# Rebuilding the head of a Fourier-mixing and leaky-ReLU kernel: even and odd rows, small first weights, a fixed order

## The chip, the cores and the metric

The kernel runs on one core of a Trainium2 chip. The metric is the device time of one execution in microseconds, as the median of several runs. Beside it there is one profiled execution, whose span goes from the first to the last instruction; all durations of single instructions come from that execution.

## The reference

The input is x of 8 batches, 3008 rows and 256 columns. It is Fourier-transformed along the rows and along the columns, the real part is kept, and the 24064 resulting rows of 256 values go through two weight matrices with a leaky ReLU between them:

```python
X = np.fft.fft(x, axis=1)
X = np.fft.fft(X, axis=2)
x = X.real.astype(np.float32).reshape(B * S, D)
h = x @ w_in                   # 256 x 2048
g = np.maximum(0.01 * h, h)
return (g @ w_out).astype(np.float32)   # 2048 x 256
```

The weights arrive as float64, everything else as float32.

## The kernel before

**Folding the transform.** Real Fourier transforms have mirror symmetries, and the kernel uses them to shrink the products. For one batch, `load_x` brings x into one tile `xt` with two halves h, two mirrored copies, seven row groups and 256 columns. The first four row groups are even rows, the last three odd rows (`NI = [4, 3]`). `fold_rows` adds the mirrored rows of one half and forms sums and differences of mirrored columns; `fold_halves` adds and subtracts the two halves. All of this is VectorE work (with a small ScalarE copy and a GpSimd memset for the edge columns). `sequence` then multiplies the folded rows with sine and cosine tables on TensorE, four products for the even rows and three for the odd rows, and `butterfly` combines the results on VectorE into `mix0` and `mix1`, the mixed activations. One such pair is a unit (batch, parity of the output row); there are 16 units, with 753 or 752 columns. Column 128 of x has no mirror, the Nyquist column: `fold_nyquist`, `nyquist` and `spread` transform it for all batches at once and send the row through DRAM to all partitions as `nb`.

**The column transform is folded into the weights.** `fold_w_in` multiplies w_in with a table, so that `wf` holds the transformed weights, and `wn`, one scalar for each hidden value, the Nyquist weights. `wn` is a row of `wf` that is turned into columns by a trip through DRAM (`spread_wn`). The float64 weights are first converted to float32 by the class `Weights`: five VectorE operations and two ScalarE operations for each tile of 128 x 512.

**The blocks.** Each unit is cut into three blocks of 251 or 250 columns, and for each block there are eight steps f over the hidden values, two hidden blocks of 128 in each. `up` makes cos_ps and sin_ps (four products), VectorE adds the Nyquist term (`cos`, lines 496 to 498), forms sum and difference (`g`, lines 500 and 501), ScalarE applies the leaky ReLU (line 502). `down` adds g times w_out into PSUM, three steps later (`lag = 3`). The first two blocks are "plain": they use w_out as it is, eight products a step (`down_plain`). All later blocks use seven products on combinations `wt` of w_out, made by `combine_w_out` on GpSimd, and combinations `s` of g, also made on GpSimd.

**The order.** A scheduler places the instructions of each engine from the order in which the program writes them; each engine then works through its list in that order. SyncE issues nearly all transfers from one queue. The head runs from line 595 on: load and convert the first and third 512 columns of w_in, fold them, send wn through DRAM, fold the Nyquist column, load and fold x of batch 0, transform unit 0; then the plain steps, two at a time, with the rest of the weights converted between them. In the plain steps of before, step f works on the hidden blocks f and 8 + f, which is why the head needs columns 0 to 511 and 1024 to 1535 first.

Of the kernel before, what the change touches and what calls it, by code (L numbers as in the profile page):

```python
# [201 lines left out]
def tile_fnet_leaky_relu(  # L202
# [24 lines left out]
    def load_x(b, q=None):  # L227
        t = xp.tile([P, 2, 2, NT, D], F32, tag="x", bufs=1, name="xt")
        for h in range(2):
            (q or nc.sync).dma_start(t[:, h], x[b, :, h])  # L230
        return t
# [3 lines left out]
    def fold_rows(t, h):  # L235


        a, z = t[:, h, 0], t[:, h, 1]
        nc.vector.tensor_tensor(a, a, z, op=ALU.add)
        lo, hi = a[:, :, 1:P], a[:, :, P + 1 : D]  # L240
        nc.vector.tensor_tensor(z[:, :, P + 1 : D], lo, hi, op=ALU.subtract)
        nc.vector.tensor_tensor(z[:, :, 1:P], lo, hi, op=ALU.add)
        nc.scalar.copy(z[:, :, 0:1], a[:, :, 0:1])
        nc.gpsimd.memset(z[:, :, P : P + 1], 0.0)

    def fold_halves(b, t):

        a, z = t[:, :, 0], t[:, :, 1]
        nc.vector.tensor_tensor(a[:, 0], z[:, 0], z[:, 1], op=ALU.add)
        nc.vector.tensor_tensor(a[:, 1], z[:, 0], z[:, 1], op=ALU.subtract)  # L250
        zs[b] = t
# [19 lines left out]

    quarters = {}
# [9 lines left out]
    wn_dram = dram.tile([2, F // 2], F32, name="wn_dram")  # L282
# [7 lines left out]
    class Weights:  # L290
# [7 lines left out]
        def __init__(self, src, dst):  # L298
            n = len(parts)
            tag, bufs = (("o", 2), ("e", 2), ("raw", 1))[n % 3]  # L300
            self.raw = work.tile([P, 2 * WN], F32, tag=tag, bufs=bufs, name="raw")
            self.dst = dst
            self.f64 = src.dtype != F32
            raw = self.raw if not self.f64 else self.raw.bitcast(src.dtype)
            nc.sync.dma_start(raw[:, 0 : src.shape[1] * src.shape[2]].rearrange("p (c n) -> p c n", c=src.shape[1]), src)  # L305
            parts.append(self)
# [4 lines left out]
        def begin(self):  # L311
            if not self.f64:
                return
            hi = self.word(I32, 1)
            self.power = work.tile([P, WN], F32, tag="power", bufs=2, name="power")
            man, power = self.dst, self.power
            man_i, power_i = man.bitcast(I32), power.bitcast(I32)
            v = nc.vector
            v.tensor_scalar(man_i, in0=hi, scalar1=0xFFFFF, scalar2=0x100000, op0=ALU.bitwise_and, op1=ALU.bitwise_or)
            v.tensor_scalar(power_i, in0=hi, scalar1=20, scalar2=0x7FF, op0=ALU.logical_shift_right, op1=ALU.bitwise_and)  # L320
            nc.scalar.activation(power, power_i, ACT.Relu, scale=-1.0, bias=inf[:, 0:1])
            nc.scalar.activation(power_i, power, ACT.Relu, scale=-(2.0**23), bias=inf[:, 1:2])

        def end(self):
            if not self.f64:
                nc.vector.tensor_copy(self.dst, self.raw[:, 0:WN])
                return
            hi, lo = self.word(I32, 1), self.word(U32, 0)
            man, power = self.dst, self.power
            man_i, power_i = man.bitcast(I32), power.bitcast(I32)  # L330
            v = nc.vector
            v.scalar_tensor_tensor(man, in0=lo, scalar=2.0**-32, in1=man_i, op0=ALU.mult, op1=ALU.add)
            v.scalar_tensor_tensor(power_i, in0=hi, scalar=-(2**31), in1=power_i, op0=ALU.bitwise_and, op1=ALU.bitwise_or)  # L333
            v.scalar_tensor_tensor(man, in0=man, scalar=2.0**-20, in1=power, op0=ALU.mult, op1=ALU.mult)
# [3 lines left out]
    def convert(made):  # L338
        for w in made:
            w.begin()  # L340
        for w in made:
            w.end()

    def load_w_in(f0):
        n, made = w_in.shape[1] // F, []
        for a in range(2):
            w = work.tile([P, WN], F32, tag="win", bufs=4, name="win")
            src = w_in[a * P : (a + 1) * P, n * f0 : n * (f0 + WN)].rearrange("p (c n) -> p c n", c=1)
            made.append(Weights(src, w))
        return made  # L350

    def fold_w_in(f0, made):

        for w in range(2):
            pt = up_ps()
            for a in range(2):
                nc.tensor.matmul(pt, lhsT=feat_sb[:, a, w * P : (w + 1) * P], rhs=made[a].dst, start=(a == 0), stop=(a == 1))  # L357
            nc.scalar.copy(wf[:, w, f0 : f0 + WN], pt)

    def spread_wn(f0):  # L360


        row = wn_dram[:, f0 : f0 + WN]
        nc.scalar.dma_start(row.rearrange("(o h) n -> o h n", o=1), wf[0:1, 1].rearrange("o (h n) -> o h n", h=2)[:, :, f0 : f0 + WN])
        at = f0 // P

        def rest():
            for h in range(2):
                nc.scalar.dma_start(wn[:, h * NH + at : h * NH + at + WN // P], row[h].rearrange("(q p) -> p q", p=P))  # L369
        return rest  # L370

    def load_w_out(f):
        made = []
        for h in range(2):
            at = (h * NH + f) * P
            src = w_out[at : at + WB * P, :].rearrange("(c p) d -> p c d", p=P)
            made.append(Weights(src, wo[:, h, f : f + WB, :].rearrange("p c d -> p (c d)")))
        return made
# [51 lines left out]
    def dft(u, blk):  # L430
# [3 lines left out]
        if c == 1:  # L434
            rows = zs[b][:, 1 - blk, 0, :, blk * P : (blk + 1) * P]
        else:
            rows = quarters.pop((b, blk))
# [12 lines left out]
    def fold_nyquist():  # L450
        nc.vector.tensor_tensor(nyb, nya, nyb, op=ALU.add)
        nc.vector.tensor_tensor(nya[:, 0], nyb[:, 0], nyb[:, 1], op=ALU.add)
        nc.vector.tensor_tensor(nya[:, 1], nyb[:, 0], nyb[:, 1], op=ALU.subtract)

    def nyquist(c):
# [8 lines left out]
        def rest():  # L464
            t = work.tile([P, UW[0]], F32, tag="mix0", bufs=2, name="nyq")
            butterfly(t, sums, B, 0, c)
            nc.sync.dma_start(nyq_dram[:, c, 0 : UW[c]], t[0:B, 0 : UW[c]])
        return rest
# [7 lines left out]


# [6 lines left out]

    def up(j, f):
        b, c, at, n, _ = blocks[j]
        pt = [up_ps("cos_ps"), up_ps("sin_ps")]
        for blk in range(2):
            for h in range(2):
                fs = slice((h * NH + f) * P, (h * NH + f + 1) * P)  # L490
                nc.tensor.matmul(pt[blk][:, h * n : (h + 1) * n], lhsT=wf[:, blk, fs],  # L491
                                 rhs=mixed[b, c][blk][:, at : at + n], start=True, stop=True)
        cos = work.tile([P, 2 * CW], F32, tag="cos", bufs=3, name="cos")
        for h in range(2):
            hs = slice(h * n, (h + 1) * n)
            nc.vector.scalar_tensor_tensor(cos[:, hs], in0=spreads[b, c][:, at : at + n],  # L496
                                           scalar=wn[:, h * NH + f : h * NH + f + 1],
# [27 lines left out]
    def down_plain(j, f):  # L525
# [4 lines left out]
        a = hidden.pop((j, f))  # L530
        for d in range(2):
            for r in range(2):
                for h in range(2):
                    nc.tensor.matmul(sums[j][d][:, r * n : (r + 1) * n], lhsT=wo[:, h, f, d * P : (d + 1) * P], rhs=a[r][h],  # L534
# [35 lines left out]
    def step(at):  # L570
        if at < len(steps):
# [6 lines left out]
            if n + 1 < len(units) and f == 4:  # L578
                if part == 0 and n > 0:
                    spread(units[n + 1])  # L580
                if part == 0:
                    if n % 2 == 1:
                        t = xs.pop(b + 1)
                        for h in range(2):
                            fold_rows(t, h)
                        fold_halves(b + 1, t)
                elif n > 0:
# [8 lines left out]
    nc.vector.memset(inf[:, 0:1], 1151.0)  # L596
    nc.vector.memset(inf[:, 1:2], 255.0 * 2.0**23)
    w0 = load_w_in(0)
    nc.sync.dma_start(feat_sb, feat_tab.rearrange("(a p) n -> p a n", p=P))
    w2 = load_w_in(2 * WN)  # L600
    nc.sync.dma_start(nyx, x_nyq)
    t0 = load_x(0)
    for n in range(4):
        load_tab(nc.sync, n, 1)
    convert(w0)
    fold_w_in(0, w0)
    convert(w2)
    fold_w_in(2 * WN, w2)
    spread_wn(0)()
    fold_nyquist()  # L610
    fold_rows(t0, 0)
    fold_rows(t0, 1)
    fold_halves(0, t0)
    nyquist(1)()
    dft(units[0], 0)()
    spread(units[0])
    dft(units[0], 1)()
# [7 lines left out]

    o = load_w_out(0)
    convert(o)
    some_steps(plain)
    w = load_w_in(WN)
    convert(w)  # L630
    fold_w_in(WN, w)
    some_steps(plain)
    w = load_w_in(3 * WN)
    convert(w)
    fold_w_in(3 * WN, w)
    spread_wn(WN)()
    some_steps(plain)
    o = load_w_out(WB)
    for n in range(4):
        load_tab(nc.sync, n, 0)  # L640
    convert(o)
    for blk in range(2):
        fold_x_quarters(0, blk)
    some_steps(plain)
    nyquist(0)()
    spread(units[1])
    for f in range(2 * WB, NH, WB):
        o = load_w_out(f)
        convert(o)
        some_steps(plain)  # L650
        dft(units[1], f // WB - 2)()
# [33 lines left out]
```

## Time and profile before

| what | value |
|---|---|
| median of 3 runs (lowest, highest) | 1936.67 us (1936.01, 1937.45) |
| span of the profiled execution | 1935.4 us |
| TensorE busy | 1909.9 us (99%) |
| VectorE busy | 1149.3 us (59%) |
| first product of a block (cos_ps) starts at | 40.4 us |
| first product with w_out (sum_ps) starts at | 47.1 us |
| moved by DMA | 73.68 MB |

In the views shown below, PE is TensorE and PEld its weight load, DVE is VectorE, ACT ScalarE, POOL GpSimd and SP SyncE. A product of float32 values shows as two records, each as wide as the moving operand. A time in a row of the chain or the timeline is the start in microseconds from the start of the span, then the length. "issue" is time in which an engine waited for nothing that the profile shows. PEclk is the granted share of the TensorE clock.

### The profile page before, as it was taken

How to read it: one execution, taken by the hardware profiler on the slowest of the kernel's cores; microseconds unless marked ns; L12 is line 12 of the kernel's file. 1: busy time of each engine (PE TensorE's matmuls, PEld its weight loads, DVE VectorE, ACT ScalarE, POOL GpSimd, SP SyncE). 2: the span in 40 equal slices, each digit the busy share in tenths (PEclk: the TensorE clock that was granted, in tenths of full speed). 3: DMA queues.
4: the chain of work that ended last, by engine and by line, in shares of the span. 5: the costliest groups of instructions: out<-in, count | busy, mean ns of one | idle time of the engine just before them, and what ended most of it. 6: DMA issues, size and time to landing. Idle time of an engine off the chain costs nothing.

```text
span 1935.4 us, 24654 instructions
## 1 busy us (share of the span) xinstructions
PE 1909.9 (99%) x8988; PEld 1687.9 (87%) x8988; DVE 1149.3 (59%) x2245; ACT 468.6 (24%) x560; POOL 1055.4 (55%) x1508
## 2 busy tenths in 40 slices
PE   5999999999999999999999999999999999999999
PEld 3888888888888888888888888888888888888888
DVE  7975555585455845567555775457645585545554
ACT  3522222222222222222222222222222222222221
POOL 0115555575555755557555665557655575555554
PEclk8999999999999999999999999999999999999999
DMA  7220000020001100020000200002000020000000
GB/s 276 63 87 30 11 20 11 22 95 11 19 22 68 39 12 30 12 88 19 22 19 11 95 20 14 19 11 96 22 11 19 11 106 11 18 13 22 11 11 22
DMA packets 25600, 73.68 MB, mean 38 GB/s; under 512 B 4596, under 2 KB 17524, under 8 KB 23432
## 3 DMA queue, kind: packets, MB, share of 16 engines
q1 hardware_dynamic: 23360, 72.09, 10.1%
q8 instruction: 72, 1.18, 0.2%
q14 instruction: 48, 0.39, 0.1%
q10 hardware_dynamic: 2120, 0.02, 0.1%
HBM read 47.38 MB, written 24.71 MB: 37 GB/s over the span
## 4 chain that ended last, share of the span: by engine, by line
PE 98%; DMA 1%; DVE 0%; issue 0%; ACT 0%; SPq 0%; ACTq 0%; DVEq 0%
PE sum_ps L554 56%; PE cos_ps L491 17%; PE sin_ps L491 17%; PE sum_ps L534 3%; PE dft_ps L412 3%; PE dft_ps L402 2%; PE up_ps L357 1%; DMA raw<-in_w_in_dram 0%; DMA wn_dram<-wf 0%; DVE power L333 0%; DVE e L565 0%; DVE cos L496 0%; ACT g L502 0%; ACTq L369 0%; SPq L305 0%
## 5 line engine op out<-in xcount | busy, mean ns | idle before, releaser
L496 DVE SCALAR_TENSOR_TENSOR cos<-nb,wn,cos_ps 128x251 f32<-128x251 f32 (+1 forms) x768 | 330.6, 472 | 682.6 <-PE cos_ps L491 682.3
L502 ACT ACTIVATE g<-g 128x1004 f32<-128x1004 f32 (+1 forms) x384 | 399.2, 1039 | 1154.4 <-DVE g L501 1102.6
L509 POOL TENSOR_TENSOR s<-g 128x251 f32<-128x251 f32 (+1 forms) x368 | 265.5, 721 | 727.1 <-ACT g L502 722.6
L554 PE MATMUL sum_ps<-s,wt 128*128 128x251 f32 (+1 forms) x2208 | 527.7, 374 | 0.0
L554 PEld LDWEIGHTS sum_ps<-s,wt 128*128 128x128 f32 x2208 | 416.3, 189 | 52.3
L491 PE MATMUL cos_ps<-mix,wf 128*128 128x251 f32 (+1 forms) x1536 | 388.1, 375 | 0.0
L491 PE MATMUL sin_ps<-mix,wf 128*128 128x251 f32 (+1 forms) x1536 | 387.7, 374 | 0.0
L554 PE MATMUL sum_ps<-g,wo 128*128 128x251 f32 (+1 forms) x1472 | 372.5, 375 | 0.0
L491 PEld LDWEIGHTS cos_ps<-mix,wf 128*128 128x128 f32 x1536 | 291.5, 190 | 36.0 <-issue 1.8
L491 PEld LDWEIGHTS sin_ps<-mix,wf 128*128 128x128 f32 x1536 | 290.6, 189 | 34.5 <-DVE mix L427 0.2
L554 PEld LDWEIGHTS sum_ps<-g,wo 128*128 128x128 f32 x1472 | 279.8, 190 | 38.4
L512 POOL TENSOR_TENSOR s<-g,s 128x251 f32<-128x251 f32 (+1 forms) x368 | 273.0, 742 | 28.9
L500 DVE TENSOR_TENSOR g<-cos,sin_ps 128x502 f32<-128x502 f32 (+1 forms) x384 | 259.5, 676 | 47.9 <-DVE cos L496 11.3
L510 POOL TENSOR_TENSOR s<-s,g 128x251 f32<-128x251 f32 (+1 forms) x368 | 271.4, 738 | 0.0
L511 POOL TENSOR_TENSOR s<-g 128x251 f32<-128x251 f32 (+1 forms) x368 | 263.6, 716 | 0.0
L501 DVE TENSOR_TENSOR g<-cos,sin_ps 128x502 f32<-128x502 f32 (+1 forms) x384 | 257.2, 670 | 0.0
L554 PE MATMUL sum_ps<-s,wo 128*128 128x251 f32 (+1 forms) x736 | 215.9, 375 | 0.0
L554 PE MATMUL sum_ps<-g,wt 128*128 128x251 f32 (+1 forms) x736 | 215.8, 375 | 0.0
L554 PEld LDWEIGHTS sum_ps<-s,wo 128*128 128x128 f32 x736 | 139.6, 190 | 16.2
L554 PEld LDWEIGHTS sum_ps<-g,wt 128*128 128x128 f32 x736 | 140.0, 190 | 15.7
L565 DVE TENSOR_TENSOR o<-e,sum_ps 128x251 f32<-128x251 f32 (+1 forms) x184 | 67.5, 408 | 8.7 <-ACT e L563 8.7
L534 PE MATMUL sum_ps<-g,wo 128*128 128x251 f32 x256 | 58.8, 383 | 2.9 <-ACT g L502 2.9
(65 smaller groups left out, 652.8 us busy)
## 6 DMA issues: line engine op xcount, KB each, us to landing
xt<-in_x_dram SPq DMA_DIRECT2D x16, 1792.0 KB, 6.8
out_dram<-o SPq DMA_DIRECT2D x80, 251.0 KB, 2.3
raw<-in_w_in_dram SPq DMA_DIRECT2D x8, 512.0 KB, 5.2
raw<-in_w_out_dram SPq DMA_DIRECT2D x8, 512.0 KB, 4.3
out_dram<-o SPq DMA_DIRECT2D x16, 250.0 KB, 2.3
nb<-nyq_dram SPq DMA_DIRECT2D x8, 376.5 KB, 3.3
nb<-nyq_dram SPq DMA_DIRECT2D x8, 376.0 KB, 4.4
tab<-in_seq_tab_dram SPq DMA_DIRECT2D x2, 564.0 KB, 13.9
```

Of the source, the lines that this page charges most:

```text
L491: nc.tensor.matmul(pt[blk][:, h * n : (h + 1) * n], lhsT=wf[:, blk, fs], rhs=mixed[b, c][blk][:, at : at + n], start=True, stop=True)
L496: nc.vector.scalar_tensor_tensor(cos[:, hs], in0=spreads[b, c][:, at : at + n], scalar=wn[:, h * NH + f : h * NH + f + 1], in1=pt[0][:, hs ...
L500: nc.vector.tensor_tensor(g[:, 0], cos[:, 0 : 2 * n], pt[1][:, 0 : 2 * n], op=ALU.add)
L501: nc.vector.tensor_tensor(g[:, 1], cos[:, 0 : 2 * n], pt[1][:, 0 : 2 * n], op=ALU.subtract)
L502: nc.scalar.activation(g, g, ACT.Lrelu)
L509: nc.gpsimd.tensor_tensor(s1, a[1][0], a[1][1], op=ALU.add)
L510: nc.gpsimd.tensor_tensor(s2, s1, a[0][0], op=ALU.subtract)
L511: nc.gpsimd.tensor_tensor(s3, a[0][0], a[1][0], op=ALU.subtract)
L512: nc.gpsimd.tensor_tensor(s4, a[0][1], s2, op=ALU.subtract)
L534: nc.tensor.matmul(sums[j][d][:, r * n : (r + 1) * n], lhsT=wo[:, h, f, d * P : (d + 1) * P], rhs=a[r][h], start=(f == 0 and r == 0 and h ...
L554: nc.tensor.matmul(sums[j][p], lhsT=still[p], rhs=moving[p], start=(f == 0 and i % 2 == 0), stop=(f == NH - 1), skip_group_check=True)
L565: nc.vector.tensor_tensor(to, x, y, op=ALU.add)
```

## The change

The head is written anew; the blocks after it keep their arithmetic.

- x of batch 0 is loaded and folded in even and odd rows apart (`load_rows`, `add_mirrors`, `fold_columns`, `fold_halves`). The half differences of part 0 go to a tile of their own, `differences`, and the half sums for the other parity are made later, among the plain steps. Later batches use `fold_x`, with four half operations in place of two.
- The first 512 columns of w_in are loaded and converted as two parts of 256; the rest in three parts of 512, one at a time. The plain steps now work on the hidden blocks 2f and 2f + 1 (`hidden_blocks`), so the columns are needed from left to right. w_out is loaded in single tiles.
- VectorE's order is the written one for the whole head and the plain steps; TensorE's and GpSimd's too until the first two steps are written (`manual_schedule`).
- `fold_nyquist` and the two transfers of `spread_wn` move to GpSimd. The first Nyquist row is spread by two products with a row of ones (`spread_first`) in place of the trip through DRAM.
- `keep_warm` writes products of a tile of zeros into PSUM: ten at the start, seven after the first weights, three after the first two steps.
- One small Lrelu at the start brings ScalarE's table in. The transforms of unit 1 move from the plain steps into block 2.

```diff
-    def fold_rows(t, h):
-        a, z = t[:, h, 0], t[:, h, 1]
-        nc.vector.tensor_tensor(a, a, z, op=ALU.add)
...
+    def add_mirrors(t, h, rows):
+        a, z = t[:, h, 0, rows], t[:, h, 1, rows]
+        nc.vector.tensor_tensor(a, a, z, op=ALU.add)
...
+    def fold_halves(t, part, c, rows, to=None):
+        i, cols = (c + part) % 2, slice(part * P, (part + 1) * P)
+        z = t[:, :, 1, rows, cols]
+        to = t[:, i, 0, rows, cols] if to is None else to[:, rows]
+        nc.vector.tensor_tensor(to, z[:, 0], z[:, 1], op=(ALU.add, ALU.subtract)[i])
...
+    def spread_wn(f0, n):
+        row = wn_dram[f0 : f0 + n]
+        nc.gpsimd.dma_start(row.rearrange("(o n) -> o n", o=1), wf[0:1, 1, f0 : f0 + n])
+        nc.gpsimd.dma_start(wn[:, f0 // P : (f0 + n) // P], row.rearrange("(q p) -> p q", p=P))
...
+    def spread_first(rows):
+        c = PARITIES[0]
+        t = work.tile([P, UW[0]], F32, tag="nb", bufs=2, name="nb")
+        for i in range(2):
+            half = slice(i * UW[c] // 2, (i + 1) * UW[c] // 2)
+            pt = dft_ps()[:, 0 : UW[c] // 2]
+            nc.tensor.matmul(pt, lhsT=one, rhs=rows[0:1, half], start=True, stop=True)
+            nc.scalar.copy(t[:, half], pt)
+        spreads[0, c] = t
...
+    def hidden_blocks(j, f):
+        return (2 * f, 2 * f + 1) if j < plain else (f, NH + f)
...
+            if n == 0 and j == plain and f in (2, 5):
+                dft(units[1], f // 5)()
...
-    w0 = load_w_in(0)
-    nc.sync.dma_start(feat_sb, feat_tab.rearrange("(a p) n -> p a n", p=P))
-    w2 = load_w_in(2 * WN)
-    nc.sync.dma_start(nyx, x_nyq)
-    t0 = load_x(0)
...
+    def keep_warm(n):
+        pt = ps.tile([P, 512], F32, tag="sum", bufs=4, name="sum_ps")
+        for _ in range(n):
+            nc.tensor.matmul(pt[:, 0 : 2 * P], lhsT=blank[:, 0:P], rhs=blank, start=True, stop=True)
+
+    with tc.manual_schedule(engines={mybir.EngineType.DVE}):
+        with tc.manual_schedule(engines={mybir.EngineType.PE, mybir.EngineType.Pool}):
...
+            w = load_w_in(0, half)
+            load_rows(0, evens)
+            nc.sync.dma_start(feat_sb, feat_tab.rearrange("(a p) n -> p a n", p=P))
+            load_rows(1, evens)
+            nc.sync.dma_start(nyx, x_nyq)
+            for n in range(2):
+                load_tab(nc.sync, n, 1)
+            for h in range(2):
+                load_rows(h, odds)
+            for n in range(2, 4):
+                load_tab(nc.sync, n, 1)
+            o = load_w_out(0)
+            keep_warm(10)
+            fold_nyquist()
+            convert_w_in(0, half, w)
+            w = load_w_in(half, half)
+            keep_warm(7)
+            differences = work.tile([P, 4 * CW], F32, tag="s", bufs=4, name="differences")[:, 0 : NT * P].rearrange("p (c d) -> p c d", c=NT)
+            nyq = nyquist(1)
+            for rows in (evens, odds):
+                for h in range(2):
+                    add_mirrors(t, h, rows)
+                    fold_columns(t, h, 0, rows)
+                    if rows == odds and h == 0:
+                        fold_columns(t, h, 1, slice(0, NT))
+                fold_halves(t, 0, 1, rows, differences)
+            fold_columns(t, 1, 1, slice(0, NT))
+            fold_halves(t, 1, 1, slice(0, NT))
...
+            rests = [nyq, dft(units[0], 0), dft(units[0], 1)]
+            spread_first(rests[0]())
+            rests[1]()
+            for part in o:
+                part.begin()
+                part.mantissa()
+            rests[2]()
+            some_steps(1)
+            for part in o:
+                part.end()
+            some_steps(1)
+            keep_warm(3)
+        convert_w_in(half, half, w)
+        o = load_w_out(1)
+        convert(o)
+        w = load_w_in(WN, WN)
+        some_steps(plain)
...
+        for q in range(2, NF // WB):
+            if q % 2 == 0:
+                f0 = q // 2 * WN
+                convert_w_in(f0, WN, w)
+            o = load_w_out(q)
+            convert(o)
+            if q % 2 == 0 and f0 + WN < F:
+                w = load_w_in(f0 + WN, WN)
+            if q == 3:
+                for part in range(2):
+                    fold_halves(t, part, 0, slice(0, NT))
+            some_steps(plain)
+            if q in (5, 7):
+                fold_x_quarters(0, q // 7)
```

## The prediction

> **What bounds the kernel now.** I read the page first: busy shares, slices, chain.
>
> ```profile
> span 1935.4 us, 24654 instructions
> PE 1909.9 (99%) x8988; PEld 1687.9 (87%) x8988; DVE 1149.3 (59%) x2245; ACT 468.6 (24%) x560; POOL 1055.4 (55%) x1508
> ...
> PE   5999999999999999999999999999999999999999
> ...
> PE 98%; DMA 1%; DVE 0%; issue 0%; ACT 0%; SPq 0%; ACTq 0%; DVEq 0%
> ```
>
> TensorE carries 98% of the chain and only the first slice (48 us) is not full. So the change, which sits in the head, can win only time in which TensorE waits or runs slowly there, and every matmul or wait that it puts behind the first full stretch costs its whole length. Next the chain in order of time over the first 60 us (start, length, what):
>
> ```profile
> 10.95 9.95 PE up_ps L357 x16
> ...
> 21.54 4.27 DMA wn_dram<-wf
> ...
> 27.14 4.33 issue
> 31.48 2.85 PE dft_ps L402 x8
> 34.33 3.34 PE dft_ps L412 x6
> 37.66 1.28 PE dft_ps L402 x8
> 38.94 1.91 PE dft_ps L412 x6
> ...
> 46.05 1.05 ACT g L502
> 47.10 0.04 issue
> 47.15 8.33 PE sum_ps L534 x30
> ```
>
> The first block product (cos_ps) starts when this transform ends, at 40.4. Then the windows table (length, then busy time of PE, PEld, DVE, ACT, POOL; granted clock; DMA share, GB/s):
>
> ```profile
> 31.40:36.90 5.50, 5.42 (x13) 4.29 (x14) 3.71 (x10) 3.65 (x9) 0.00 (x0) 0.50 0.49 141
> 36.90:40.30 3.40, 3.40 (x15) 2.48 (x15) 2.58 (x6) 1.91 (x3) 0.00 (x0) 0.97 0.29 103
> 40.30:44.10 3.80, 3.80 (x18) 2.95 (x16) 3.46 (x8) 0.29 (x1) 0.73 (x1) 1.00 0.71 246
> 44.10:47.10 3.00, 0.18 (x1) 0.00 (x0) 3.00 (x7) 1.04 (x1) 2.09 (x3) 1.00 0.92 304
> 47.10:50.80 3.70, 3.65 (x9) 3.00 (x10) 3.70 (x10) 2.85 (x5) 0.00 (x0) 0.54 0.14 53
> 50.80:55.10 4.30, 4.30 (x21) 3.81 (x21) 4.30 (x9) 1.56 (x4) 0.00 (x0) 1.00 0.41 141
> ```
>
> After its start at 40.4 TensorE loses 3.0 us waiting for the first g and some 1.8 us at clock 0.54 (9 products where 4.30 us hold 21). From 50.8 on no row shows a gap.
>
> [...] clock 0.50 at 31.4 after the idle stretch from 23.4, 0.54 at 47.1 after 3.0 us of waiting. [...]
>
> **The change, part by part**, as times in the new span. Landings come from the two x transfers of before (a timeline row, and the foot of the view of tile xt), issued at 3.6 and 4.6:
>
> ```profile
> 3.59 1.98 SPq L230 DMA_DIRECT2D xt<-in_x_dram  x2
> ```
> ```profile
> DMA to landing us min/median/max: 11.0/12.6/14.3
> ```
>
> That is 4208 KB of queue at 14.6 and 6000 KB at 18.9, 2.4 us per 1000 KB. The new queue (weights 512 KB, even rows 1024, table 256, even rows 1024, nyx 112, two tables 940, odd rows twice 768) puts even rows at 8.2 and 11.3, tables at 13.8, odd rows at 15.6 and 17.5.
>
> VectorE: 1792 elements step 1.93 us, 889 step 1.0, so 1024 take 1.13, 768 0.86, 508 0.59, 381 or 384 0.46. The first weights are half as wide as before, where the first pair landed at 4.2 and 6.3 and was converted by 11; I put them at 3.6 and 4.4, and their ten operations (two of 0.20 and three of 0.34 each, from 0.34 and 0.61 at 512) with ScalarE's two steps between at 7.0, before the first even rows. Even rows: 8.2 + 1.13 + 0.59 = 9.9; 11.3 + 1.72 = 13.0; first half sums 13.6. Odd rows: 15.6 + 1.32 = 16.9; differences of columns 17.9; second half (landed) + 1.32 = 19.2; half sums 19.7; + 1.0 + 1.0 = 21.7. TensorE has the Nyquist transform (16.8) and the first part's transform done by 21.6, each standing for its rows. Then the Nyquist butterfly, four operations stepping 0.27, 0.26, 0.46, 0.46, to 23.2, which frees the PSUM bank for the second part of the last transform: six products of 376 at 0.314 = 1.9, 25.1; two row broadcasts (four records) 1.26, so the first cos_ps stands at **26.4**, against 40.4: 14.0 gained. The half sums for parity 0 leave this path (2.0 us, later under full TensorE), and the ScalarE wait behind the wn transfers (the 4.27 and 4.33 rows) goes with their move to GpSimd. The zero products before it run while TensorE has nothing, and end before 14; GpSimd's Nyquist fold lies beside the odd rows' landing. [...]
>
> Work after the first cos_ps: 1935.4 - 40.4 = 1895.0, less 3.0 and 1.8, is 1890.2. Added: before folds two of four 512-wide weight parts after its start (16 records at 0.43 = 6.9); the new head folds one of 256 and three of 512 there (8 x 0.213 + 24 x 0.43 = 12.0). That is +5.1. Three zero products add 6 x 0.213 = 1.3.
>
> The new waits. Each weight part runs convert, fold, wf copy, wn to DRAM and back, and only then cos; VectorE's order is fixed, so all later conversions stand behind that wait. The old second pair shows the price on ScalarE's queue (timeline, then the foot of the view of tile wn): 1.73 to the read's issue, 2.2 to landing.
>
> ```profile
> 67.36 0.58 ACTq L364 DMA_DIRECT2D wn_dram<-wf  x1
> ...
> 69.09 0.92 ACTq L369 DMA_DIRECT2D wn<-wn_dram  x2
> ```
> ```profile
> DMA to landing us min/median/max: 2.2/4.3/5.3
> ```
>
> Second part: the g of step 1 needs VectorE to 32.7, its Lrelu (1.04) to 33.7, four half-width power steps on ScalarE behind it to about 35.6, VectorE to 36.7; fold 38.3, second wf copy 39.1. The read is queued on GpSimd behind a difference of w_out that waits for the second w_out conversion (41.1, plus 0.73): 41.8. wn lands at 44.0 to 44.4 (2.2[...]). Two cos operations 0.78, two sums 1.18, Lrelu 1.05: g at 47.1 to 47.5. TensorE meanwhile: four ups 3.4 to 29.8, zero products 31.1, 13 sums 36.6, fold 38.3, ups 41.7, three sums 43.0. It waits 4.1 to 4.5 and then runs cold, 1.8 again. Third part (512 wide): 6.8 us of sums and ups cover the chain, 0.3 left. Then 1.5 for step 6, whose VectorE work stands behind a w_out conversion and the moved half sums. Fourth: only 1.3 us of sums behind the ups, 1.1 to 1.9 of waiting; fifth: none, 2.0 to 2.9. Sum 1.3 + 0.1 + 4.1 + 1.8 + 0.3 + 1.5 + 1.1 + 2.0 = 12.2, or 14.3 at the upper prices; I take 12.7, near the measured price. So 26.4 + 1890.2 + 5.1 + 12.7 = 1934.4 (1.3 stands in the waits). The renamed hidden blocks change no count; the transforms of unit 1, moved into block 2, and folding later x in four half sums of 896 in place of two of 1792 lie under TensorE. A timed run stands 1.3 over this span (1936.67 against 1935.4): **1935.7 us**.
>
> **The rivals.** *The waits stay short (faster).* If wn comes back before the w_out conversion ends, the first wait is 1.1 and leaves the clock up (4.8 less), and the fourth and fifth go (3.1 less): 1927.8; half of it 1931.8. For it: 1.1 to 2.9 us are small against my precision. Against: both wn transfers must then take under 2 us together.
>
> *The wn round trip on GpSimd becomes the bound (slower).* The first pair of before, beside 400 GB/s of loads, took 4.27 and up to 5.3, 9.6 in place of 3.9. At +3 us in three places and a second cold stretch it ends near 1946; it decides from +1.6 us in each. For it: loads of w_in and w_out queue at the same time[...]. Against: DMA share in the old 50 to 80 is only 0.25 to 0.33.
>
> *It doesn't do what it says.* If zero products leave the clock low, 1.9 + 1.3 of head products and 3.4 of ups run at half rate: some 6.5 more, 1942.
>
> **How the numbers follow.** 0.2% (3.9 us) is about what can be told from no change. The forecast, gain of the start eaten by folds and waits, has 0.41 (its own range 1933 to 1940.4); the short waits 0.32; the slow round trip 0.20; cold zeros 0.07. So faster 0.32, same 0.41, slower 0.27. The range 1928 to 1942 takes in the short waits' floor nearly, and the cold zeros; the slow trip's far end is left out. x landing a microsecond off moves the end by as much and is inside.
>
> **What would show it.** First cos_ps at 26.4 (25 to 28.5); last odd row fold ended by its landing; TensorE idle before the third g near 43, ended by ScalarE, the cos before it ended by the wn transfer; clock 0.5 just after; short gaps on cos_ps at the fourth and fifth parts; work after the start longer by 5. The forecast is wrong if wn is never the releaser, if the start is past 30, or if a gap appears after 130.

## The result, and the profile after

| | before | changed |
|---|---|---|
| median of the runs (lowest, highest) | 1936.49 us (1936.01, 1937.45) | 1950.99 us (1950.07, 1953.49) |
| span of the profiled execution | 1935.4 us | 1948.1 us |
| first cos_ps product starts | 40.7 us | 28.3 us |
| from there to the last TensorE record | 1890 us | 1915 us |

The changed kernel is slower: ratio 1.0076, 95% interval 1.0059 to 1.0094. The forecast was 1935.7 us with a range from 1928 to 1942. The head did nearly what was forecast of it: it is 12.4 us shorter. (The first product's own record starts at 40.7 in the kernel before; the 40.4 given earlier is the start of its weight load.) The loss is 25 us after the head, all before 135 us.

Two words are used from here on. The weights w_in come in five parts, in the order of their columns: 256, 256, and three times 512. A round is the conversion of one w_out tile and two steps f behind it. Here is the page, from its first lines to the shares of the chain:

```profile
span 1948.1 us, 24808 instructions
PE 1925.0 (99%) x9040; PEld 1696.9 (87%) x9040; DVE 1159.6 (60%) x2273; ACT 471.0 (24%) x570; POOL 1070.5 (55%) x1523
...
PE   8899999999999999999999999999999999999999
...
PE 95%; DVE 2%; DMA 1%; ACT 0%; POOL 0%; issue 0%; SPq 0%; DVEq 0%
```

One digit shows it, if one knows where to look: the second slice (49 to 97 us) was 9 before and is 8 now, and the chain has fallen from 98% TensorE to 95%. The "99% busy" line hides it: a product at half clock counts as busy (3.41 of 3.41 us in the rows at 0.50 below), and 17 us are 1% of the span. Who ended TensorE's waits after its start (total us, times, longest):

```profile
PE cos_ps L526 <- DVE cos L531: 8.0, 3, 3.3
PE sum_ps L569 <- ACT g L537: 5.3, 2, 4.9
```

Both names only pass a delay on. The view of tile wn says what VectorE waited for before its cos operations, 22.4 us in four times, one for each weight part after the first:

```profile
  DMA wn<-wn_dram: 22.4, 4
```

The chain in order of time shows the four trips of wn, to DRAM and back, each with what stood in it:

```profile
43.31 0.72 POOL wt L402
44.03 0.15 issue
44.18 2.59 DMA wn<-wn_dram
...
60.34 4.83 DMA wn_dram<-wf
65.17 0.28 issue
65.45 2.57 DMA wn<-wn_dram
...
92.45 2.04 POOL wt L402 x3
94.49 2.65 DMA wn<-wn_dram
...
121.02 0.53 POOL wn_dram L388
121.56 0.80 POOL wt L402 x2
122.36 0.57 issue
122.93 0.67 POOL wt L402
123.59 2.57 DMA wn<-wn_dram
```

In three of the four, a w_out difference (L402) stands on GpSimd ahead of the read; in the other, the write alone needs 4.83 us. Last, the table of windows (length, busy time of PE, PEld, DVE, ACT, POOL, granted clock, DMA share, GB/s) for the 3.41 us around the end of each wait and the 3.41 us after them, four times:

```profile
47.05:50.46 3.41, 0.22 (x1) 0.22 (x2) 3.20 (x7) 1.04 (x1) 0.00 (x0) 1.00 0.00 0
50.46:53.87 3.41, 3.41 (x9) 2.76 (x9) 3.41 (x9) 2.55 (x4) 0.00 (x0) 0.50 0.00 0
67.53:70.94 3.41, 1.55 (x6) 1.13 (x7) 2.71 (x6) 0.55 (x1) 0.00 (x0) 1.00 0.00 0
70.94:74.35 3.41, 3.41 (x10) 2.73 (x9) 2.72 (x6) 2.27 (x4) 0.00 (x0) 0.50 0.00 0
94.83:98.25 3.42, 1.38 (x8) 0.89 (x6) 0.91 (x3) 0.00 (x0) 0.46 (x1) 1.00 0.03 1
98.25:101.66 3.41, 3.41 (x9) 2.71 (x10) 3.31 (x7) 1.05 (x2) 0.00 (x0) 0.50 0.00 0
125.55:128.97 3.42, 1.44 (x6) 1.01 (x7) 2.60 (x6) 0.44 (x1) 0.00 (x0) 1.00 0.01 0
128.97:132.38 3.41, 3.41 (x10) 2.75 (x9) 2.84 (x6) 2.28 (x4) 0.00 (x0) 0.50 0.00 0
```

Nine or ten records stand in 3.41 us where sixteen would fit (a full-rate record steps 0.21): after each of the four waits the clock was granted at 0.5 for 3.413 us, which costs 1.7 us each time. The waits sum to 17.3 us against 3.1 before (14.2 more), counted from the start of one TensorE record to the start of the next, less the full-rate step. (The view of waits, which counts from a modelled end, gives 14.0 against 2.9.) With three more cold stretches (5.1), the folds that moved behind the start (5.1) and the zero products (1.3), these terms come to 25.7, a little more than the 25 that were lost.

### The profile page after: what moved, and what is told of

The parts are those of the page before. It is cut to its first block, busy times and chain, and to the rows that moved or that the text cites. A ratio compares the mean times of both kernels' runs of the same rounds, so it can differ in the third digit from the quotient of the medians.

```text
span 1948.1 us, 24808 instructions
## 1 busy us (share of the span) xinstructions
PE 1925.0 (99%) x9040; PEld 1696.9 (87%) x9040; DVE 1159.6 (60%) x2273; ACT 471.0 (24%) x570; POOL 1070.5 (55%) x1523
## 4 chain that ended last, share of the span: by engine, by line
PE 95%; DVE 2%; DMA 1%; ACT 0%; POOL 0%; issue 0%; SPq 0%; DVEq 0%
PE sum_ps L589 56%; PE sin_ps L526 16%; PE cos_ps L526 16%; PE dft_ps L429 3%; PE dft_ps L419 2%; PE sum_ps L569 2%; DMA wn<-wn_dram 1%; DMA xt<-in_x_dram 1%; PE up_ps L382 0%; DVE cos L531 0%; DMA wn_dram<-wf 0%; DVE g L535 0%; POOL wt L402 0%; DVE g L536 0%; DVE power L357 0%
## 5 line engine op out<-in xcount | busy, mean ns | idle before, releaser
L547 POOL TENSOR_TENSOR s<-g,s 128x251 f32<-128x251 f32 (+1 forms) x368 | 271.4, 737 | 28.8
L545 POOL TENSOR_TENSOR s<-s,g 128x251 f32<-128x251 f32 (+1 forms) x368 | 276.0, 750 | 0.0
```

The source lines that it names most:

```text
L545: nc.gpsimd.tensor_tensor(s2, s1, a[0][0], op=ALU.subtract)
L547: nc.gpsimd.tensor_tensor(s4, a[0][1], s2, op=ALU.subtract)
```

## The experiments

The theory is that the trip of wn through DRAM is issued right before its use and stands on the path four times, and that each wait costs a cold stretch besides. The rivals were named A (VectorE's fixed order and the weight conversion bound it), B (the load of the transfers), C (the w_out differences in GpSimd's queue), D (GpSimd's queue is slow in itself) and E (on the zero products). "Cold" is the time at clock 0.5 after the first cos_ps product, without the last few us of a run.

| kernel | median us | ratio to before, 95% | first cos_ps | cold us |
|---|---|---|---|---|
| changed | 1950.99 | 1.0059 to 1.0094 | 28.3 | 13.7 |
| wn from TensorE | 1938.04 | 1.0002 to 1.0019 | 28.3 | 0 |
| wn left out | 1930.80 | 0.9961 to 0.9983 | 28.9 | 0 |
| GpSimd's order written out | 1948.80 | 1.0046 to 1.0076 | 29.2 | 17.1 |
| wn on ScalarE's queue | 1941.25 | 1.0016 to 1.0032 | 28.9 | 3.4 |
| first part 512 wide | 1944.55 | 1.0026 to 1.0055 | 29.3 | 10.2 |
| each part one round ahead | 1928.41 | 0.9942 to 0.9972 | 29.4 | 0 |
| no zero products | 1949.65 | 1.0050 to 1.0080 | 28.8 | 13.7 |
| free VectorE order later | 1947.45 | 1.0031 to 1.0064 | 31.6 | 13.7 |
| wn with one hop more | 1963.42 | 1.0123 to 1.0157 | 32.1 | 17.1 |
| before, wn on GpSimd | 1934.91 | 0.9985 to 1.0002 | 37.6 | 6.8 |
| ahead, wn on ScalarE | 1929.11 | 0.9948 to 0.9977 | 30.0 | 0 |
| ahead, no zero products | 1927.39 | 0.9938 to 0.9968 | 29.2 | 0 |

**wn from TensorE.**

```diff
+        for q in range(n // P):
+            for a in range(2):
+                nc.tensor.matmul(pt[:, q : q + 1], lhsT=made[a].dst[:, q * P : (q + 1) * P], rhs=feat_sb[:, a, P : P + 1], start=(a == 0), stop=(a == 1))
+        nc.scalar.copy(wn[:, f0 // P : (f0 + n) // P], pt)
...
-        spread_wn(f0, n)
+        make_wn(f0, n, made)
```

> The wn columns come from TensorE: for each hidden block two products of the converted w_in with the one Nyquist column of the table (128 x 1 results), and one small ScalarE copy; no trip through DRAM. Theory (the trip stands on the path four times and each wait drops TensorE's clock for 3.4 us): of the 17.3 us in which TensorE is idle after the first block product some 13.8 go, of the four cold stretches (6.8 us) at least three, and the 32 small products with their weight loads cost about 2: 1931 to 1935 us, first block product unchanged near 28. Rival A (VectorE's fixed order and the weight conversion are the bound, wn is only the last to come): the same gaps come back ended by VectorE conversions, above 1944. Rival B (the loads of weights crowd everything in 40 to 130): gaps and cold stretches stay, 1948 or more.

1938.04 us, 3 above the expected range. The waits for wn and all cold stretches are gone, as the theory said, and rivals A and B fall: nothing ended by a conversion took the waits' place. But the products cost far more than the 2 us expected. Rows after the start, from the groups of lines (busy, mean ns, idle before):

```profile
L389 PE MATMUL wn_ps<-feat_sb,win 128*128 128x1 f32 x56 | 6.5, 244 | 0.0
L389 PEld LDWEIGHTS wn_ps<-feat_sb,win 128*128 128x128 f32 x56 | 6.9, 192 | 1.5 <-issue 1.4
```

Each of the 56 records with one moving column has a load of 128 x 128 weights beside it, 192 ns on average. In the chain 16 records take 1.68 us, 0.105 each, so the 56 take 5.9. That is 3.9 more than was expected, which makes up for the miss.

**wn left out.**

```diff
+            nc.gpsimd.memset(wn, 0.05)
...
-        spread_wn(f0, n)
```

> The Nyquist weights are left out: wn is a constant set once, so no trip and no products stand for it. All else is the changed kernel. Theory: 1929 to 1933, a little under the kernel with wn from TensorE; what idle time stays after the first block product (near 3 us) is ended by conversions. Rival A (conversion and fixed VectorE order are the bound): above 1944. Rival B (load on the DMA queues): 1948 or more.

1930.80 us, inside the range. So the trip costs the changed kernel 20.2 us (1950.99 - 1930.80), waits and cold stretches together, and without it the new head would win 0.3%.

**GpSimd's order written out.** The differences are written behind the read.

```diff
-    with tc.manual_schedule(engines={mybir.EngineType.DVE}):
-        with tc.manual_schedule(engines={mybir.EngineType.PE, mybir.EngineType.Pool}):
+    with tc.manual_schedule(engines={mybir.EngineType.DVE, mybir.EngineType.Pool}):
+        with tc.manual_schedule(engines={mybir.EngineType.PE}):
...
             convert(o)
+            if q > 3:
+                combine_w_out((q - 4) * WB)
```

> Only GpSimd's order is changed: it is the written one until the end of the plain steps, so that each wn read stands directly behind its wn write and the w_out differences come after it. Theory (the latency of the trip itself is the cost): the read of the second part is issued some 0.8 us earlier, of the fourth and fifth 0.5 each, the third not at all; all four waits and cold stretches stay: 1948 to 1950. Rival C (the w_out differences ahead of the read are the cost): the waits shrink to under 2 us and the clock stays up: under 1942.

1948.80 us: 2.2 us better, and rival C falls. This is a small part of the 20, and only 0.9 us lie between the slowest of its runs and the fastest of the changed kernel's. Its chain, second and third part:

```profile
42.47 2.14 DMA wn_dram<-wf
44.61 0.28 issue
44.89 2.86 DMA wn<-wn_dram
...
61.65 5.07 DMA wn_dram<-wf
66.72 0.28 issue
67.00 2.55 DMA wn<-wn_dram
```

**wn on ScalarE's queue.**

```diff
-        nc.gpsimd.dma_start(row.rearrange("(o n) -> o n", o=1), wf[0:1, 1, f0 : f0 + n])
-        nc.gpsimd.dma_start(wn[:, f0 // P : (f0 + n) // P], row.rearrange("(q p) -> p q", p=P))
+        nc.scalar.dma_start(row.rearrange("(o n) -> o n", o=1), wf[0:1, 1, f0 : f0 + n])
+        nc.scalar.dma_start(wn[:, f0 // P : (f0 + n) // P], row.rearrange("(q p) -> p q", p=P))
```

> The two transfers of each part are issued by ScalarE, as in the kernel before, in place of GpSimd; nothing else. Theory (any trip through DRAM at this place is on the path): the second part's wn comes 1 to 2 us earlier because no w_out difference is ahead of the read, but ScalarE stands still between write and read and delays the leaky ReLU of the step before; waits of 2 to 4 us and most cold stretches stay: 1943 to 1950. Rival D (GpSimd's queue is what is slow): the waits go under 1 us and the time to 1936 or less.

1941.25 us, better than the theory allowed and worse than rival D: leaving GpSimd's queue takes away about half. It saves 9.7 of the 20.2 us (1950.99 - 1941.25), and three cold stretches fewer (5.1) and the missing w_out differences ahead of the read (2.2 at most, by the run above) are in this; the other 10.5 are what a trip on ScalarE costs at this place. The same two parts in its chain:

```profile
41.89 1.88 DMA wn_dram<-wf
43.77 0.02 issue
43.79 3.04 DMA wn<-wn_dram
...
60.12 2.53 DMA wn_dram<-wf
62.67 2.18 DMA wn<-wn_dram
```

In the third part a w_out tile of 512 KB is loading beside the write, in all three kernels (issued at 59.8 here and in the changed kernel, at 61.0 in the one with GpSimd's order written out). GpSimd's write takes 4.83 us in the changed kernel and 5.07 with its order written out, ScalarE's 2.53. The second part still waits for 4.2 us and runs cold; the later waits shrink to 2.1 us and less and leave the clock up.

**The first part 512 wide again**, so that there is no second half part.

```diff
-            w = load_w_in(0, half)
+            w = load_w_in(0, WN)
...
-        convert_w_in(half, half, w)
         o = load_w_out(1)
```

> Undoes one part: the first w_in part is 512 columns wide again, so there is no second half part; wn still goes through DRAM on GpSimd's queue for every part. Theory (each wn trip costs its wait plus a cold stretch): the wait at the second step (5.1 us) and its cold stretch (1.7) go, its fold (1.7) moves ahead of the first block product; against that the head starts later by about 2 (VectorE converts 4 us longer before the even rows, of which 2.3 were idle). The three later waits stay: 1942 to 1947. Rival A (conversion is the bound): the wait moves to the w_out conversion at the same place, 1949 or more.

1944.55 us, the middle of the range. No TensorE wait is left before 58 us. The start moved only 1.1 us and not 2: VectorE now converts in time in which it had waited for the even rows (0.97 and 1.26 us in the changed kernel). The 1.1 come later, where VectorE's last differences wait 1.04 us for a copy by ScalarE.

**Each part one round ahead.** As the last one, and the parts are converted, folded and sent in rounds 1, 3 and 5 in place of 2, 4 and 6.

```diff
-        convert_w_in(half, half, w)
+        convert_w_in(WN, WN, w)
         o = load_w_out(1)
         convert(o)
-        w = load_w_in(WN, WN)
+        w = load_w_in(2 * WN, WN)
...
-            if q % 2 == 0:
-                f0 = q // 2 * WN
+            if q % 2 == 1 and q < 7:
+                f0 = (q + 1) // 2 * WN
                 convert_w_in(f0, WN, w)
...
-            if q % 2 == 0 and f0 + WN < F:
+            if q % 2 == 1 and f0 + WN < F:
```

> As the kernel with the first part 512 wide, and each later part of w_in is converted, folded and sent through DRAM one round of two steps earlier, so the trip has two steps to come back in; the trip itself is unchanged, on GpSimd's queue. Theory (the trip costs only because it is issued right before its use): the three remaining waits (10.4 us with their tails) and three cold stretches (5.1) go, a new wait of 1 to 2 us at the second step comes in, because VectorE then has w_in and w_out to convert before it: 1929 to 1934, and the wn read is on the releasing side of no TensorE wait. Rival A (VectorE's order and conversion are the bound): 1940 or more. Rival D (GpSimd's queue is slow in itself and delays whatever stands behind it): above 1938, with waits on GpSimd.

1928.41 us, 0.6 below the range: faster than both kernels, with the same trips on the same queue. The new wait of 1 to 2 us at the second step, which was expected, did not come. In the view of tile wn (what ended idle time before its instructions) the read of wn releases VectorE no more (the last row is the read itself, which waits for its write):

```profile
  PE cos_ps L526: 661.5, 273
  DMA tab<-in_seq_tab_dram: 4.4, 1
  DMA wn_dram<-wf: 3.7, 2
```

This run decides between the theory and rival D: a trip that is issued a round of two steps ahead costs nothing that shows, though the first two behind the start take 5.8 and 6.2 us here from the write's issue to the read's landing. Against the kernel with the wide first part alone it gains 16.1 us. The edit moves the conversions ahead along with the trip; that the trip is what counted rests on this run together with the two above in which the conversions stay and the trip goes.

**No zero products.**

```diff
-            keep_warm(10)
-            keep_warm(7)
-            keep_warm(3)
```

> All twenty zero products are left out; nothing else. Theory: they hold TensorE's clock up in the head, so without them the Nyquist transform and the transform of unit 0 run at 0.5 and the first block product starts 2 to 4 us later; the last three (1.3 us) no longer stand on the path; the four wn waits stay: 1951 to 1954. Rival E (zero products do nothing for the clock): the first block product stays at 28 and the time is 1949 to 1950.

1949.65 us: the theory was wrong here. Rival E's number came out (1949 to 1950), but not its reason, because the clock did stay low longer: it is granted at 1.0 from 17 us, from 6 with the zero products. The first cos_ps came at 28.8 us, only 0.5 later and not 2 to 4, since little more than the first half of the Nyquist transform ran cold. From the chain:

```profile
13.61 2.67 PE dft_ps L419 x8
16.28 2.29 PE dft_ps L429 x6
18.57 1.49 PE dft_ps L419 x8
```

Eight records at half clock take 2.67, eight of the same width 1.49 later. This delays a copy by ScalarE, and so VectorE's last differences, by half a microsecond; for the rest TensorE has to wait for VectorE anyway (1.2 us). The last three zero products had stood where TensorE now waits 1.3 us. The difference to the changed kernel is within the spread (1947.03 to 1950.80 against 1950.07 to 1953.49).

**Free VectorE order later.** The written order holds only to the first two steps.

```diff
-    with tc.manual_schedule(engines={mybir.EngineType.DVE}):
+    if True:
-        with tc.manual_schedule(engines={mybir.EngineType.PE, mybir.EngineType.Pool}):
+        with tc.manual_schedule(engines={mybir.EngineType.PE, mybir.EngineType.DVE, mybir.EngineType.Pool}):
```

> VectorE's order is written out only up to the first two steps and is the scheduler's after that; nothing else. Theory (no g can be made before wn is back, in whatever order): TensorE still waits at the four places, with little less: 1945 to 1951. Rival A (the fixed VectorE order holds up work that could go on): 1938 or less.

1947.45 us: rival A falls again, since 1938 is far off. The waits are fewer and longer (11.9 us against 14.0 in the same view), and the start came 3.3 us later, which is not explained here. What the fixed order is worth by itself is not shown by this run, whose times spread from 1942.67 to 1948.54:

```profile
PE cos_ps L526 <- DVE cos L531: 8.0, 1, 8.0
PE up_ps L382 <- DVE cos L531: 3.9, 1, 3.9
```

**One hop more for wn.**

```diff
-        nc.gpsimd.dma_start(wn[:, f0 // P : (f0 + n) // P], row.rearrange("(q p) -> p q", p=P))
+        copy = wn_copy[f0 : f0 + n]
+        nc.gpsimd.dma_start(copy.rearrange("(o n) -> o n", o=1), row.rearrange("(o n) -> o n", o=1))
+        nc.gpsimd.dma_start(wn[:, f0 // P : (f0 + n) // P], copy.rearrange("(q p) -> p q", p=P))
```

> The changed kernel with one more hop for wn: row to DRAM, DRAM to DRAM, DRAM to columns, all on GpSimd's queue; nothing else. Theory (the trip stands on the path four times in full length): a hop costs 2 to 3 us (1.6 us of landing in the quiet parts, up to 2.6, and its issue), so four more of them make 1959 to 1965. Rival A (VectorE's order and conversion are the bound and wn only comes last by little): 1951 to 1954.

1963.42 us, inside the range, but by luck, as the sum is another one. VectorE's waits for wn grew from 22.4 to 29.9 us, 1.9 for each hop, and one cold stretch was added; 3.9 us came in the head, where x landed 1.3 later and the transform ran cold. It supports the direction, not the price.

**The kernel before with wn on GpSimd.**

```diff
-        nc.scalar.dma_start(row.rearrange("(o h) n -> o h n", o=1), wf[0:1, 1].rearrange("o (h n) -> o h n", h=2)[:, :, f0 : f0 + WN])
+        nc.gpsimd.dma_start(row.rearrange("(o h) n -> o h n", o=1), wf[0:1, 1].rearrange("o (h n) -> o h n", h=2)[:, :, f0 : f0 + WN])
...
-                nc.scalar.dma_start(wn[:, h * NH + at : h * NH + at + WN // P], row[h].rearrange("(q p) -> p q", p=P))
+                nc.gpsimd.dma_start(wn[:, h * NH + at : h * NH + at + WN // P], row[h].rearrange("(q p) -> p q", p=P))
```

> The kernel before with one part of the change alone: its two wn trips are issued by GpSimd in place of ScalarE. Theory (a trip's queue matters only where the trip is on the path; in the kernel before it is issued long before its use): ScalarE no longer stands between write and read in the head, VectorE's idle 1.9 us before the half sums goes, so 1.5 to 2 us are gained: 1934 to 1936. Rival D (GpSimd's queue is slow in itself): 1938 or more.

1934.91 us; the interval touches 1, so a small gain at best. The first product starts some 3 us earlier, and a cold stretch of 6.8 in place of 3.4 us, after a wait of the same 3.1 us, gives 1.7 of it back. In this kernel, where the trip has time, GpSimd's queue costs nothing that shows.

**One round ahead, on ScalarE's queue, and without zero products.** Two kernels, the edits as above.

> The kernel that converts each w_in part one round ahead, with the wn transfers issued by ScalarE. Theory: the trip is hidden, so its queue no longer matters: 1927 to 1930, against 1928.4 with GpSimd's queue. Rival D: GpSimd's queue still costs, 1925 or less.

1929.11 us: no difference, once the trip is hidden.

> The kernel that converts each w_in part one round ahead, without the twenty zero products. Theory (the head waits for VectorE's folds, so a cold start of the Nyquist transform is hidden, and the last three stand in a wait): 1927 to 1930, no difference. Rival E (they pay by holding the clock): 1931 or more.

1927.39 us: the best version, 0.5% under before and 1.2% under the changed kernel, and the zero products are not needed.

## Why the prediction was wrong

Its own formula was start + 1890.2 + 5.1 + waits = span, with 26.4 for the start and 12.7 for waits, cold clock and zero products together. The span of 1948.1 with the measured start leaves 24.5 for the last term: 28.3 + 1890.2 + 5.1 + 24.5. Measured one by one its pieces are 17.3 of waits, 6.8 of cold clock and 1.3 of zero products, 25.4. Of the difference, 0.3 is in the 1890.2, which counts from the weight load at 40.4 and not from the first product at 40.7; the other 0.6 stays open.

- **The start, 28.3 for 26.4.** Landing was nearly right (15.94 for 15.6). The VectorE chain was done with the last odd differences at 20.6 for 19.7. Then the prediction had a step wrong: it let the even products of the transform's second part run in the time before. But one VectorE operation (L256, 128 x 896) makes the half sums of all seven row groups, even ones too, and it ran at 21.7 to 22.8; so the even products began at 23.4 and stand on the path (1.51):

```profile
5.64 10.28 DMA xt<-in_x_dram
...
20.05 0.57 DVE differences L256
...
20.66 2.16 PE dft_ps L429 x6
22.82 0.58 issue
23.41 1.51 PE dft_ps L419 x8
24.92 1.90 PE dft_ps L429 x6
26.82 1.46 PE dft_ps L504 x4
```

  The last odd-row fold was not ended by its landing either, but by VectorE itself. The start is 1.9 of the 13.7 us that the span missed by.
- **The failed step: the price of the trip, and a clock charged once.** The waits by part, forecast and measured: second 4.1 to 4.5, was 5.1; third 0.3, was 3.6; step 6 1.5, was 0.7; fourth 1.1 to 1.9, was 2.7; fifth 2.0 to 2.9, was 4.1; another 1.0 at the third part's folds was not foreseen. Together this is 17.3 us where the forecast had some 10, and the third part is the largest miss. The mechanism was right, wn coming last behind VectorE's cos, and the sizes were wrong. The trip was priced at 3.9 to 4.3 us, from a quiet pair on ScalarE's queue. ScalarE can do it faster still (1.13 + 2.10 in the quiet fifth part of the run on its queue). On GpSimd the same part takes 0.28 + 1.59 + 0.28 + 2.56 = 4.7 with nothing in its way (in the kernel with GpSimd's order written out), and the third part of the changed kernel takes 0.28 + 4.83 + 0.28 + 2.57 = 8.0. The prediction also found the w_out difference ahead of the read in the second part, but did not carry it to the fourth and fifth.
- **The cold clock, 1.8 for 6.8.** The prediction charged the wait of 4.1 us alone. That its own waits of 0.3 to 2.9 us in the later parts would leave the clock up was its estimate, which the profile of before does not show. The trace of the changed kernel shows otherwise: from 94.83 to 98.25 TensorE was busy for 1.38 of 3.42 us, and the clock was 0.50 for the 3.41 after it. With the third and fifth parts that makes three more stretches, 5.1 us.
- **The third part.** "6.8 us of sums and ups cover the chain" left out that the write itself can need the 4.83 us that it took here beside a 512 KB load.
- **Right:** that TensorE's idle time starts before the third g and is ended by ScalarE (45.0 rather than near 43), that wn is behind it, the gaps at the later parts, the +5.1 for folds, that nothing is lost after 135 us, and that GpSimd's Nyquist fold lies beside the odd rows' landing (it ran from 11.8 to 13.9 us, after waiting for its input to land).
- **The rivals.** The second one, the round trip on GpSimd becoming the bound, comes nearest to what happened; it had 0.20. It was sized with +3 us in three places and two cold stretches, 1946, and its far end was left out of the range; it came in four places with four. But it is GpSimd's queue only by about half: on ScalarE's queue the trip still costs 10.5 us. The first rival (short waits) needed both transfers under 2 us together; the fastest pair seen here, on ScalarE, took 3.2. The third (cold zeros) is refuted: in the changed kernel the clock was at 1.0 from 6 us, behind zero products alone.
- **The upper prices**, 0.4 us more for a trip on GpSimd, were the author's estimate, which no run before the result shows. Measured afterwards, the read in the fifth part landed in 2.56 us on GpSimd's queue (its order written out) and in 2.10 on ScalarE's. The 0.28 us before each step and the slow write beside the load (4.83 against 2.53) come on top, and they are most of the difference.

Open: why GpSimd's write takes 4.8 to 5.1 us beside a load that leaves ScalarE's at 2.5. Work of VectorE at the same time is an unlikely cause: VectorE was busy 0.15 us of the 4.83, and 0.05 us of the 5.07 in the kernel with GpSimd's order written out. Taking the load away was not tried. A small slip of the prediction stays besides: it set a timed run 1.3 us above the span by comparing a median (1936.67) with the span of another execution. All runs here stand 1.7 to 2.2 us above their own span, before too (1.8), so the forecast was 0.5 us low for this reason.

## What to carry to other kernels

When an edit moves a small transfer next to its use, price the whole path (engine queue, issue, write, wait, read) on the queue and under the load that it will have, and multiply by the number of places. Then ask of every TensorE wait of 2 us or more whether it costs the clock as well: here one of 2.0 us was followed by 3.41 us at half clock, and one of 2.6 us was not. The cure was not a faster trip but an earlier one: issuing it one round ahead, with the first part wide enough to need no second one at once, took back 22.6 us with the same transfers.

## What the runs showed of the hardware

- The changes of the granted clock lie whole numbers of steps of 3.413 us apart in both traces, of before and of the changed kernel. In the changed kernel the cold stretches begin at 50.46, 70.94, 98.25 and 128.97, which are 6, 8 and 9 such steps apart, and last one step; in the kernel before one lasts three (26.62 to 36.86) and one lasts one (47.10 to 50.51). A cold stretch after a wait went along with how busy TensorE was within one such step, more than with how long the wait was. The four steps shown above with 0.22 to 1.55 us busy were each followed by a cold one. Two with 1.54 and 1.49 us in the kernel with the 512-wide part were not:

```profile
57.04:60.46 3.42, 1.54 (x8) 1.03 (x6) 0.24 (x1) 0.00 (x0) 0.80 (x1) 1.00 0.08 1
70.69:74.11 3.42, 1.49 (x7) 0.97 (x6) 3.21 (x8) 1.81 (x4) 0.00 (x0) 1.00 0.05 16
```

  In the two traces of before and of the changed kernel, without the last few us of each, six full-clock steps were followed by half clock: with TensorE busy for 0.94 and 0.59 us before, and for 0.22, 1.55, 1.38 and 1.44 us in the changed kernel. No step with 1.75 us or more was. Between 1.49 and 1.55 us it went both ways, and the ends of TensorE's records are modelled, so these figures give no sharp edge. A wait of 2.0 us, inside one step, cost 1.7 us more (at 96.1 in the changed kernel), and one of 2.6 us, split over two steps, cost nothing more (at 58.6 in the kernel with the 512-wide part).
- With the zero products the clock was granted at 1.0 from 6 us, without them from 17. In the changed kernel TensorE had done nothing else up to 6.09 us: twelve of their records took 4.99 us, 0.42 each, and the ten after that 2.04 us, 0.20 each. Without them eight records of the Nyquist transform took 2.67 us from 13.61 on, and eight of the same width 1.49 us from 18.57 on.
- Small transfers on GpSimd's queue landed in 1.6 us (2 KB to DRAM) and 2.6 us (back) in quiet parts (the changed kernel, and the one with GpSimd's order written out), on ScalarE's in 1.13 and 2.10 (wn on ScalarE's queue, fifth part). Beside a 512 KB load the write took 4.8 to 5.1 us on GpSimd's queue and 2.5 on ScalarE's.
- Where a w_out difference stood ahead of the read on GpSimd, the read was issued behind it: in the changed kernel the read of wn for the second part at 44.18, the difference from 43.31 to 44.03; with the differences written behind the read it was issued at 44.89, 0.28 us after its write had landed at 44.61, with no difference between.
- ScalarE loaded a table twice in the kernel before, at 0.74 and 39.31, for 1.28 us each, and once in the changed kernel, at 0.74.
- A 128 x 128 by 128 x 1 float32 product took 0.21 us in two records (16 records in 1.68 us, wn from TensorE), as against 0.43 for a moving width of 251: half the price for 251 times less to move.
